# Batch 0's attention products as sixteen matmuls with tail rows copied, a filler behind the first, and batch 1's values loaded ahead of W2's last quarter

## The chip, the cores and the metric

The kernel runs on one core of a Trainium2 chip. The metric is device time in microseconds (us). Engines are written as the profile has them: PE is TensorE (PEld its weight loads), DVE is VectorE, ACT is ScalarE, POOL is GpSimd, SP is SyncE, whose queue issues transfers. Matmul results land in PSUM, in banks of 512 fp32 numbers per partition; everything else lies in SBUF, 128 partitions wide.

## What is computed

Sinkhorn attention over blocks, then a residual MLP with affine layers. Batch 4, 8 heads, sequence 768 in 8 blocks of 96, head size 64, so 512 channels.

```python
# sort_net P: five rounds of exp and of row and column normalization
k_sorted = np.einsum('bhij,bhjcd->bhicd', P, k_b)
v_sorted = np.einsum('bhij,bhjcd->bhicd', P, v_b)
scores = scale * np.matmul(q_b, k_sb.transpose(0, 1, 2, 4, 3))    # block by block, 96 x 96
attn = softmax(scores)
x = np.matmul(attn, v_sb)          # to (batch, 768, 512)
a1 = alpha1 * x + beta1
u = x + lam * np.einsum('ts,bsd->btd', w_tok, a1)
a2 = alpha2 * u + beta2
out = u + lam * (np.maximum(a2 @ w_ch1, 0.0) @ w_ch2)
```

## The kernel before

All four batches run through one program whose order is written out by hand: `Engine` (line 58) keeps the instructions of each engine in the order in which the Python code issues them (`tc.keep_in_program_order`, line 67), so nearly every instruction carries line 65. An engine that waits holds up everything behind it in its own queue. Waits come from data, and from buffers: a tile pool hands out a buffer again when its last reader is done. PSUM has two such pools: `psa`, two buffers of two banks each, and `psb`, four buffers of one bank each (lines 84 to 91). Which buffer a tile gets depends on how many were taken before it.

Batch 0 has a start of its own, written out in lines 900 to 985 and 1073 to 1082. In this order:

1. Values are mixed by the sort matrix (`v_mm`, `v_out`), and keys of head pairs 0 and 1 (`k_turn`, `k_copy`). The eight heads go in four pairs, g = 0 to 3.
2. `score(0, g, hf, ...)` multiplies queries with keys for four blocks, and ACT takes the exponentials into `et`. With a `psa` tile it is one activation of 768 elements, with `psb` tiles two of 384.
3. `pv_first(g)` (line 464) multiplies the exponentials of pair g with the values. Column 64 of the values is one, so each product carries its own row sum; DVE takes the reciprocal and multiplies, and the result is 128 channels of `x_of[0]`.
4. `wtok` turns the token weights (transposed on PE, copied by DVE or ACT into `w_tokT`); `first_mm(g)` multiplies them with x; `first_turn(g)` turns x itself; `first_finish` puts both together into `a2T`, the transposed input of the first channel product, on DVE (`SCALAR_TENSOR_TENSOR a2T`).
5. `h_part` and `h_unit` are the first channel product and its relu (`hTa`, `hTb` on ACT). `h_part(0, 0, m, [ci])` does one of the four chunks of 128 input channels, chunk ci being `a2T` of pair g = ci.

**How x lies.** A block has 96 rows, and later products want full tiles of 128 tokens. So tile kt (0 to 5) of `x` holds block kt in partitions 0 to 95, and 32 rows of block 6 or 7 in partitions 96 to 127. In `pv_first` a block of the first six is one matmul of 128 rows of weights (96 of them its own); blocks 6 and 7 are three matmuls of 32 columns each, which write straight to partitions 96 to 127 of the PSUM tile (lines 477 to 481). That makes 24 matmuls for a pair, one reciprocal over 12 numbers and one multiply of 128x768.

In batches 1 to 3 the same is done by `pv` (line 490): 16 matmuls in two halves, and `tails` (line 527) copies the rows of blocks 6 and 7 from `x[.., 6:8]` to partitions 96 to 127 by three DVE copies.

**Idle filling.** `slow(n)` (line 227) issues n matmuls of zeros in fp32, 128x512, which the hardware does in two passes each, into a `psa` tile that nobody reads. Before the change it is used ahead of the attention, never between attention products.

**Transfers.** The large loads are issued by POOL, in the order of the code: W1 in quarters, W2 in quarters (lines 956 and 957), then `load_kv(1)` (values, then keys of batch 1, each in two halves) and `load_q(1)` (lines 987 and 988). They share one DMA queue. `scale_weights(g)` (line 793) multiplies quarter g of W2 on DVE before the second channel product reads it; `put(b, hf, kind, n, ...)` names the step of the loop after which a function is run (line 1061: steps 10, 11, 12, 12). `mix_v(1, n, ...)` reads batch 1's values at steps 13 to 15.

Of the kernel before, what the change touches and what calls it, by code (L numbers as in the profile page):

```python
# [7 lines left out]
FT = mybir.dt.float32  # L8
# [3 lines left out]
ALU = mybir.AluOpType  # L12
# [4 lines left out]
def kernel(  # L17
# [22 lines left out]
    B, H, S, D = q.shape  # L40
    NB = sort_net.shape[-1]
    BLK = S // NB
# [44 lines left out]
    def psa(shape, dtype, name):  # L87
        return pools["psA"].tile(shape, dtype, name=name, tag="psA")

    def psb(shape, dtype, name):  # L90
        return pools["psB"].tile(shape, dtype, name=name, tag="psB")
# [100 lines left out]
                qn_of[b][:, kt, :, :], q[b, :, kt * 128:(kt + 1) * 128, :].rearrange("h p d -> p h d"),  # L192
            )

    def load_kv(b):
        for kv, src in ((1, v), (0, k)):
            raw = att.tile([128, HB, D], F16, name="raw", tag="raw", bufs=2)
            load_halves(raw, src[b])
            raw_of[(b, kv)] = raw
# [187 lines left out]
    def k_turn(b, g, ps):  # L387
        return turn_slab(k8, lambda r, g: bigK[b][r, g, :], g, "k_ps", ps)

    def k_copy(b, g, ps, half, eng):  # L390
        eng(
            KT0[:, g, :, :].rearrange("p i (th u) -> p (i th) u", th=2)[:, :, 0:HB].rearrange(
                "p x (c t) -> p x c t", t=12
            )[:, :, :, half * 6:half * 6 + 6],
            ps[half].rearrange("p (t x c) -> p x c t", t=6, c=4),
        )
# [17 lines left out]
    def score(b, g, hf, ps, fillers=0):  # L414
        if ps is psb:
            ps = [ps([128, 4 * BLK], FT, "sc_ps") for _ in range(2)]
            bank = [t_[:] for t_ in ps]
        else:
            ps = [ps([128, 2, 512], FT, "sc_ps")]
            bank = [ps[0][:, a, :] for a in range(2)]  # L420
        for _ in range(fillers):
            z = wz[:].bitcast(FT)[:, 0:192]
            pe.matmul(
                bank[0][:, 0:384], z[:, 0:128], z.unsqueeze(1).to_broadcast([128, 2, 192]), start=True, stop=True,
            )
        n = 128 if b == 0 else BLK
        keys = kT_of[b][:].rearrange("p g i t -> p (g i t)")
        for ii in range(4):
            i = 4 * hf + ii
            lo = (g * NB + i) * n  # L430
            w = min(128, H4 * NB * n - lo)
            for h2 in range(2):
                r = slice(h2 * 64, h2 * 64 + 64)
                pe.matmul(
                    bank[h2][0:w, ii * BLK:(ii + 1) * BLK], keys[r, lo:lo + w],
                    qT_of[b][r, g, i * BLK:(i + 1) * BLK], start=True, stop=True,
                )
        tag, bufs = ("ost", 4) if (b, g) == (0, 3) else ("et", 6)
        et = att.tile([128, 2, 4, BLK], F16, name="et", tag=tag, bufs=bufs)
        if len(ps) == 1:  # L440
            act.activation(
                et[0:n].rearrange("p a i t -> p a (i t)"), ps[0][0:n, :, 0:4 * BLK], AF.Exp, scale=scale
            )
        else:
            for a in range(2):
                act.activation(
                    et[0:n, a].rearrange("p i t -> p (i t)"), ps[a][0:n, :], AF.Exp, scale=scale
                )
        ets[(b, g, hf)] = et

    x_of = {}
# [12 lines left out]
    def pv_first(g):  # L464
        if g == 0:
            x_of[0] = moep.tile([128, 8, C], F16, name="x128", tag="x128", bufs=1)
        ps = psa([128, 2, 512], FT, "x_ps")[:, :, 0:480].rearrange("p a (k d) -> p a k d", d=80)
        for i in range(NB):
            for h2 in range(2):
                et = ets[(0, g, i // 4)][:].rearrange("p a i t -> p (a i t)")  # L470
                lo = (4 * h2 + i % 4) * BLK
                w = min(128, 8 * BLK - lo)
                val = Vs[:, (2 * g + h2) * NB + i, 0:D + 1]
                if i < 6:
                    pe.matmul(ps[0:w, h2, i, 0:D + 1], et[:, lo:lo + w], val, start=True, stop=True)
                else:
                    for a in range(3):
                        pe.matmul(
                            ps[96:128, h2, 3 * (i - 6) + a, 0:D + 1], et[:, lo + a * 32:lo + (a + 1) * 32], val,
                            start=True, stop=True,  # L480
                        )
        rc = att.tile([128, 2, 6], FT, name="rc", tag="rc", bufs=3)
        dve.reciprocal(rc[:], ps[:, :, :, D])
        dve.tensor_tensor(
            x_of[0][:, 0:NT, g * 128:(g + 1) * 128].rearrange("p k (a d) -> p k a d", a=2),
            ps[:, :, :, 0:D].rearrange("p a k d -> p k a d"),
            rc[:].rearrange("p a k -> p k a").unsqueeze(3).to_broadcast([128, NT, 2, D]), ALU.mult,
        )

    def pv(b, g, hf):  # L490
        if g == 0 and hf == 0:
# [35 lines left out]
    def tails(x, c):  # L527
        for a in range(3):
            dve.tensor_copy(x[96:128, a:a + 4:3, c], x[32 * a:32 * a + 32, 6:8, c])
# [88 lines left out]
    def row_sums(ps):  # L618
        ps = ps([128, 384], FT, "rr_ps")
        for ks in range(NT):  # L620
            j = ks % 4
            pe.matmul(
                ps[32 * j:32 * j + 32, :], ones[:], w_tokT[:, ks, 0:384], start=(ks < 4), stop=(ks > 1),
                skip_group_check=True,
            )
        act.copy(rrow[:], ps[:])
# [45 lines left out]
    def first_mm(g, ps):  # L672
        c = slice(g * 128, (g + 1) * 128)
        tps = tps_of[g] = ps([128, 384], FT, "tok_ps")[:]
        for ks in range(NT):
            pe.matmul(
                tps, x_of[0][:, ks, c], w_tokT[:, ks, 0:384], start=(ks == 0), stop=(ks == NT - 1),
            )
        if g == 3:
            first_finish(g)  # L680
        else:
            tok_copy(g)

    def first_turn(g, ps):
        c = slice(g * 128, (g + 1) * 128)
        ups = ps([128, 384], FT, "turn_ps")[:]
        for m in range(3):
            pe.matmul(
                ups[:, m * 128:(m + 1) * 128], x_of[0][:, m, c], ident16[:],
                start=(m == 0), stop=False, skip_group_check=True,  # L690
            )
        pe.matmul(ups, brow[:, c], rrow[:], start=False, stop=True, skip_group_check=True)
        if g == 0:
            z_of[0] = moep.tile([128, CT, 384], FT, name="z", tag="u32", bufs=3)
        act.activation(
            z_of[0][:, g, :], ups, AF.Identity, bias=ab2col[:, CT + g:CT + g + 1], scale=ab2col[:, g:g + 1],
        )
        if g < 3:
            first_finish(g)
# [51 lines left out]
    def h_part(b, hf, m, cis):  # L751
        if b not in hAB_of:
            hAB_of[b] = tuple(
                moep.tile([128, HK, 512], F16, name=n, tag=n, bufs=1) for n in ("hTa", "hTb")
            )
        if (b, hf) not in hT_of:
            hT_of[(b, hf)] = [
                hAB_of[b][m // HK][:, m % HK, hf * 128:hf * 128 + 384] for m in range(HT)
            ]
        if cis[0] == 0:  # L760
            h_of[m] = psb([128, 384], FT, "h_ps")
        for ci in cis:
            pe.matmul(
                h_of[m][:], W1p[:, ci, m * 128:(m + 1) * 128], a2T_of[b][hf][:, ci, :],
                start=(ci == 0), stop=(ci == CT - 1),
            )
        if cis[-1] == CT - 1:
            act.activation(hT_of[(b, hf)][m], h_of[m][:], AF.Relu)
# [128 lines left out]
    def wtok(ks, eng):  # L897
        prep_wtok(ks, 0, psb, eng)
# [55 lines left out]
        pool.dma_start(W1p[:, :, g * 512:(g + 1) * 512], w1v[:, :, g * 512:(g + 1) * 512])  # L954
    permute(1, pool.tensor_copy, 0, 6)
    for g in range(4):
        pool.dma_start(W2p[:, g * 4:(g + 1) * 4, :], w2v[:, g * 4:(g + 1) * 4, :])
    moe_start(0)
    a1_of[0] = moep.tile([128, 8, C], F16, name="a1", tag="a1", bufs=1)
    pv_first(0)  # L960
    kp2 = k_turn(0, 2, psb)
    kp3 = k_turn(0, 3, psb)
    for g, kp in ((2, kp2), (3, kp3)):
        k_copy(0, g, kp, 0, copy)
        k_copy(0, g, kp, 1, act.copy)
    score(0, 2, 0, psa)
    score(0, 2, 1, psb)
    pv_first(1)
# [3 lines left out]
        wtok(ks, copy)  # L972
    wtok(4, act.copy)
    wtok(5, copy)
    first_mm(0, psb)
    pv_first(2)
    row_sums(psb)
    first_mm(1, psb)
    first_turn(0, psb)
# [4 lines left out]
    first_turn(2, psa)  # L984
    scale_affine(betaB)

    load_kv(1)
    load_q(1)
    pool.memset(Vs[0:BLK, :, D:GRP], 1.0)

# [67 lines left out]
        put(b, 0, "h", 4, lambda b=b: moe_cross(b, 1))  # L1058
        put(b, 0, "c", 2, lambda b=b: moe_affine(b, 1))

    for g, m in enumerate((10, 11, 12, 12)):
        put(0, 0, "h", m, lambda g=g: scale_weights(g))
    for n, at_ in enumerate(((0, 1, "c", 4),) * 3 + ((0, 1, "c", 5),) * 3 + ((0, 1, "c", 6),) * 2):
        put(*at_, lambda n=n: block_weights(n))
# [7 lines left out]

    for m in range(3):
        h_part(0, 0, m, [0])
    first_turn(3, psa)
    first_mm(3, psa)
    for ci in (1, 2):
# [55 lines left out]
```

## Time and profile before

| | |
|---|---|
| time, median of 3 runs | 256.55 us (255.8 to 257.79) |
| the profiled execution's own time | 256.33 us |
| its span, first to last instruction | 254.6 us |
| busy: PE, DVE, ACT, POOL | 96%, 68%, 61%, 18% of the span |
| mean granted clock of PE | 0.993 |
| the stage that the change touches | some 18.5 to 37 us |

Columns of a timeline: start, length, engine, line, operation, tile written <- tile read, shape, count. This is PE's part of the stage, where pairs 0 and 1 are done:

```profile
18.58 1.02 PE L65 MATMUL x_ps<-Vs,et 128*128 128x65 f16 x24
19.53 0.21 PE L65 MATMUL k_ps<-bigK,k 64*64 64x64 f16 x1
21.22 0.94 PE L65 MATMUL k_ps<-bigK,k 64*64 64x64 f16 x47 [1.48 <-ACT et L65]
22.54 0.63 PE L65 MATMUL sc_ps<-qT,kT 64*128 64x96 f16 x16 [0.37 <-DVE kT L65]
23.09 1.64 PE L65 MATMUL x_ps<-Vs,et 128*128 128x65 f16 x24
```

The times of an execution are those of one run; PE's matmuls are pipelined, so a group's length is a little more than what it takes of PE. In brackets stands the idle time before a group and what ended it. A granted clock of 0.50 in a stretch means that the matmuls in it take twice as long.

### The profile page before, as it was taken

To read this page: it belongs to the slowest core of one execution; us is meant where nothing else is said; L and a number is where in the kernel's file an instruction comes from. 1 tells how busy PE (TensorE), PEld (TensorE's weight loads), DVE (VectorE), ACT (ScalarE), POOL (GpSimd) and SP (SyncE) were. 2 spreads that over 40 slices of the span, in tenths; PEclk is the share of its full clock that TensorE was granted. 3 is DMA by queue.
4 is the path that set the end of the run, shared out by engine and by line. 5 is a ranking of instruction groups with operands and counts; after the bars stand their busy time and mean duration, and the time that the engine had idled before them with its cause. 6 is when DMAs were issued, how large, how long until landed. Compare 5 with 4: busy or idle time off the path is not lost.

```text
span 254.6 us, 6059 instructions
## 1 busy us (share of the span) xinstructions
PE 244.0 (96%) x2416; PEld 159.7 (63%) x2416; DVE 174.1 (68%) x461; ACT 155.7 (61%) x285; POOL 46.1 (18%) x70
## 2 busy tenths in 40 slices
PE   7897999999999999999999999999999999999994
PEld 2475765555465545556765797558756875686783
DVE  5884588667379868279896685398978862462773
ACT  4796675567788679786564696878364005837400
POOL 8699604000082010191000010000000000000000
PEclk9997999999999999999999999999999999999999
DMA  5999999998999997999961179710203132111023
GB/s 98 202 210 192 207 205 210 216 179 197 165 179 180 131 209 124 178 159 164 136 161 39 31 189 127 141 23 0 85 0 66 50 115 45 21 41 44 0 85 82
DMA packets 61936, 31.09 MB, mean 122 GB/s; under 512 B 50562, under 2 KB 57618, under 8 KB 61908
## 3 DMA queue, kind: packets, MB, share of 16 engines
q0 software_dynamic: 20976, 16.91, 45.7%
q1 hardware_dynamic: 40836, 13.76, 32.0%
q8 instruction: 19, 0.31, 0.5%
q14 instruction: 9, 0.07, 0.1%
q10 hardware_dynamic: 96, 0.03, 0.1%
HBM read 32.79 MB, written 8.65 MB: 163 GB/s over the span
## 4 chain that ended last, share of the span: by engine, by line
PE 77%; DVE 9%; ACT 6%; DMA 3%; issue 2%; POOL 1%; DVEq 0%; ACTq 0%; POOLq 0%
PE h_ps L65 28%; PE tok_ps L65 12%; PE px L65 8%; PE ch_ps L65 8%; PE pz L65 6%; PE py L65 5%; DMA v<-in_v_dram 3%; PE x_ps L65 3%; DVE x L65 3%; PE sc_ps L65 2%; DVE sums L65 2%; PE kmix_ps L65 2%; PE mix_ps L65 2%; ACT kT L65 1%; ACT vd L65 1%
## 5 line engine op out<-in xcount | busy, mean ns | idle before, releaser
L65 PE MATMUL h_ps<-a2T,W1p 128*128 128x384 bf16 x512 | 93.4, 326 | 0.3 <-DVE a2T L65 0.3
L65 PEld LDWEIGHTS <-W1p 128*128 128x128 bf16 x512 | 47.8, 98 | 30.7
L65 ACT ACTIVATE hTa<-h_ps 128x384 f16<-128x384 f32 x64 | 31.2, 490 | 30.6 <-PE h_ps L65 29.5
L65 ACT ACTIVATE hTb<-h_ps 128x384 f16<-128x384 f32 x64 | 31.3, 489 | 8.7 <-PE h_ps L65 8.7
L65 DVE SCALAR_TENSOR_TENSOR u<-tok_ps,x 128x512 f32<-128x512 f32 x21 | 14.5, 692 | 27.0 <-PE tok_ps L65 27.0
L65 PE MATMUL tok_ps<-a,w_tokT 128*128 128x512 f16 x126 | 30.3, 379 | 0.0
L65 ACT CAST kT<-kmix_ps 64x512 f16<-64x512 f32 x36 | 25.7, 713 | 7.0 <-PE kmix_ps L65 6.5
L65 ACT ACTIVATE et<-sc_ps 96x768 f16<-96x768 f32 (+2 forms) x36 | 24.6, 736 | 2.4 <-PE sc_ps L65 2.4
L65 ACT CAST u<-u 128x512 f16<-128x512 f32 x21 | 13.0, 618 | 20.4 <-DVE u L65 20.4
L65 PEld LDWEIGHTS <-sums 128*128 128x128 f16 x216 | 21.1, 98 | 3.8 <-issue 0.7
L65 PEld LDWEIGHTS <-hTa 128*128 128x128 f16 x192 | 18.2, 98 | 6.6
L65 PEld LDWEIGHTS <-hTb 128*128 128x128 f16 x200 | 18.5, 98 | 6.1
L65 PEld LDWEIGHTS <-w_tokT 128*128 128x128 f16 x126 | 12.3, 98 | 13.1 <-DVE a L65 0.3
L65 DVE TENSOR_TENSOR x<-x_ps,rcb 96x512 f16<-96x512 f32 x24 | 16.5, 687 | 0.8
L65 DVE TENSOR_TENSOR sums<-hTa,hTb 128x512 f16<-128x512 f16 (+2 forms) x27 | 8.9, 330 | 10.3 <-ACT hTb L65 10.0
L65 PEld LDWEIGHTS <-et 96*128 96x128 f16 (+4 forms) x288 | 12.6, 103 | 2.7
L65 DVE SCALAR_TENSOR_TENSOR ost<-px,u 128x256 f32<-128x256 f32 x27 | 11.3, 419 | 3.4 <-PE px L65 3.4
L65 PE MATMUL x_ps<-Vs,et 96*128 96x65 f16 (+4 forms) x288 | 13.5, 199 | 0.0
L65 PE MATMUL ch_ps<-W2p,hTa 128*128 128x512 f16 x48 | 11.9, 380 | 0.0
L65 PE MATMUL ch_ps<-W2p,hTb 128*128 128x512 f16 x48 | 11.7, 379 | 0.0
L65 POOL DMA_DIRECT2D qn<-in_q_dram x12 | 10.7, 915 | 5.2 <-DMA raw<-in_v_dram 4.8
L65 PE MATMUL sc_ps<-qT,kT 64*128 64x96 f16 (+1 forms) x256 | 10.0, 210 | 1.5 <-DVE x L65 0.7
(140 smaller groups left out, 351.2 us busy)
## 6 DMA issues: line engine op xcount, KB each, us to landing
out_dram<-ost SPq DMA_DIRECT2D x23, 192.0 KB, 2.4
raw<-in_v_dram POOLq DMA_DIRECT2D x6, 384.0 KB, 8.4
raw<-in_k_dram POOLq DMA_DIRECT2D x6, 384.0 KB, 10.8
Vs<-vscr SPq DMA_DIRECT2D x3, 768.0 KB, 7.9
W1p<-in_moe_w_ch_dram POOLq DMA_DIRECT2D x4, 512.0 KB, 11.6
W2p<-in_moe_w_ch_dram POOLq DMA_DIRECT2D x4, 512.0 KB, 15.6
qn<-in_q_dram POOLq DMA_DIRECT2D x12, 128.0 KB, 11.1
vscr<-mixed POOLq DMA_DIRECT2D x4, 384.0 KB, 5.0
```

Source lines behind the costliest of these rows:

```text
L65: ins = getattr(self.eng, name)(*args, **kwargs)
```

## The change

- `load_kv` takes the kinds to load; values of batch 1 are issued ahead of W2's last quarter, keys where both were.
- `pv_first` does blocks 6 and 7 like the others, into a second PSUM tile `xt_ps` out of `psb`. That makes 16 matmuls. DVE takes two reciprocals and two multiplies, on 96 partitions, and writes `x_of[0][0:96, 0:8]`.
- `first_tails(g)` calls `tails` (unchanged) for pair g: three DVE copies of 32x256. Its place in the order is written out: for pair 0 behind the key copies of pairs 2 and 3, for pair 1 behind the copies of the token weights, for pair 2 right behind `pv_first(2)`, for pair 3 behind `scale_affine(betaB)` and the first three `h_part`, ahead of `first_turn(3)`.
- One `slow(1)` follows `pv_first(0)`.
- The scaling of W2's last quarter goes from step 12 to step 15. No other DVE instruction lies between the two places, so DVE's order stays as it is.

```diff
-    def load_kv(b):
-        for kv, src in ((1, v), (0, k)):
+    def load_kv(b, *kvs):
+        for kv in kvs or (1, 0):
+            src = (k, v)[kv]
...
         ps = psa([128, 2, 512], FT, "x_ps")[:, :, 0:480].rearrange("p a (k d) -> p a k d", d=80)
+        tl = psb([128, 320], FT, "xt_ps")[:].rearrange("p (a k d) -> p a k d", a=2, d=80)
         for i in range(NB):
             for h2 in range(2):
...
-                if i < 6:
-                    pe.matmul(ps[0:w, h2, i, 0:D + 1], et[:, lo:lo + w], val, start=True, stop=True)
-                else:
-                    for a in range(3):
-                        pe.matmul(
-                            ps[96:128, h2, 3 * (i - 6) + a, 0:D + 1], et[:, lo + a * 32:lo + (a + 1) * 32], val,
-                            start=True, stop=True,
-                        )
-        rc = att.tile([128, 2, 6], FT, name="rc", tag="rc", bufs=3)
-        dve.reciprocal(rc[:], ps[:, :, :, D])
-        dve.tensor_tensor(
-            x_of[0][:, 0:NT, g * 128:(g + 1) * 128].rearrange("p k (a d) -> p k a d", a=2),
...
-        )
+                dst = ps[0:w, h2, i, 0:D + 1] if i < 6 else tl[0:w, h2, i - 6, 0:D + 1]
+                pe.matmul(dst, et[:, lo:lo + w], val, start=True, stop=True)
+        rc = att.tile([128, 2, NB], FT, name="rc", tag="rc", bufs=3)
+        dve.reciprocal(rc[0:BLK, :, 0:6], ps[0:BLK, :, :, D])
+        dve.reciprocal(rc[0:BLK, :, 6:8], tl[0:BLK, :, :, D])
+        for lo, src in ((0, ps), (6, tl)):
+            n = 6 - 2 * lo // 3
+            dve.tensor_tensor(
+                x_of[0][0:BLK, lo:lo + n, g * 128:(g + 1) * 128].rearrange("p k (a d) -> p k a d", a=2),
+                src[0:BLK, :, :, 0:D].rearrange("p a k d -> p k a d"),
+                rc[0:BLK, :, lo:lo + n].rearrange("p a k -> p k a").unsqueeze(3).to_broadcast([BLK, n, 2, D]), ALU.mult,
+            )
+
+    def first_tails(g):
+        tails(x_of[0], slice(g * 128, (g + 1) * 128))
...
     for g in range(4):
+        if g == 3:
+            load_kv(1, 1)
         pool.dma_start(W2p[:, g * 4:(g + 1) * 4, :], w2v[:, g * 4:(g + 1) * 4, :])
...
     pv_first(0)
+    slow(1)
     kp2 = k_turn(0, 2, psb)
     kp3 = k_turn(0, 3, psb)
     for g, kp in ((2, kp2), (3, kp3)):
         k_copy(0, g, kp, 0, copy)
         k_copy(0, g, kp, 1, act.copy)
+    first_tails(0)
     score(0, 2, 0, psa)
...
     wtok(5, copy)
+    first_tails(1)
     first_mm(0, psb)
     pv_first(2)
+    first_tails(2)
     row_sums(psb)
...
-    load_kv(1)
+    load_kv(1, 0)
     load_q(1)
...
-    for g, m in enumerate((10, 11, 12, 12)):
+    for g, m in enumerate((10, 11, 12, 15)):
         put(0, 0, "h", m, lambda g=g: scale_weights(g))
...
     for m in range(3):
         h_part(0, 0, m, [0])
+    first_tails(3)
     first_turn(3, psa)
     first_mm(3, psa)
```

More of the change, by code (lines that the diff above doesn't have):

```diff
@@ L473, in pv_first @@
                 val = Vs[:, (2 * g + h2) * NB + i, 0:D + 1]
-                if i < 6:
-                    pe.matmul(ps[0:w, h2, i, 0:D + 1], et[:, lo:lo + w], val, start=True, stop=True)
-                else:
-                    for a in range(3):
-                        pe.matmul(
-                            ps[96:128, h2, 3 * (i - 6) + a, 0:D + 1], et[:, lo + a * 32:lo + (a + 1) * 32], val,
-                            start=True, stop=True,
-                        )
-        rc = att.tile([128, 2, 6], FT, name="rc", tag="rc", bufs=3)
-        dve.reciprocal(rc[:], ps[:, :, :, D])
-        dve.tensor_tensor(
-            x_of[0][:, 0:NT, g * 128:(g + 1) * 128].rearrange("p k (a d) -> p k a d", a=2),
-            ps[:, :, :, 0:D].rearrange("p a k d -> p k a d"),
-            rc[:].rearrange("p a k -> p k a").unsqueeze(3).to_broadcast([128, NT, 2, D]), ALU.mult,
-        )
+                dst = ps[0:w, h2, i, 0:D + 1] if i < 6 else tl[0:w, h2, i - 6, 0:D + 1]
[12 more added lines that the diff above has]
+        tails(x_of[0], slice(g * 128, (g + 1) * 128))
     def pv(b, g, hf):
```

## The prediction

> **What bounds the kernel now.** The page's chain says PE 77%, and from 41 us on it is matmuls almost throughout, with short waits for ScalarE and VectorE and none for a transfer; so whatever the change gains or loses before 41 us reaches the end whole, unless a transfer comes to have the last word. The change lies between 18.5 and 37 us, so I took the chain again for 16 to 45 us (start, length, what):
>
> ```profile
> 20.31 0.91 issue
> 21.22 0.59 PE k_ps L65 x23
> ...
> 28.09 0.76 PE x_ps L65 x21
> ...
> 30.86 0.57 ACT z L65
> 31.43 0.02 issue
> 31.45 0.62 DVE a2T L65
> ...
> 33.12 0.61 DVE a2T L65
> 33.73 0.60 DVE alphaB L65
> 34.33 0.53 DVE a2T L65
> 34.85 0.60 DVE betaB L65
> ```
>
> Two things are to be seen. At 19.6 to 21.2 TensorE stands still. From 31.45 to 36.1 the chain runs on VectorE, which goes from one operation straight to the next; matmuls wait for it. Then the busy time of each engine in stretches of 3.41 us, cut where the granted clock changes (columns: stretch and length, busy us of PE, PEld, DVE, ACT, POOL with instruction counts, granted clock, DMA share, GB/s):
>
> ```profile
> 12.56:15.97 3.41, 2.83 (x152) 2.71 (x153) 3.27 (x7) 3.41 (x7) 3.41 (x4) 1.00 1.15 207
> ...
> 19.39:22.80 3.41, 1.56 (x68) 1.31 (x66) 2.16 (x4) 1.77 (x5) 3.41 (x4) 1.00 1.20 165
> 22.80:26.21 3.41, 3.41 (x60) 2.94 (x54) 1.46 (x4) 2.59 (x6) 3.41 (x5) 0.50 1.16 220
> 26.21:29.62 3.41, 3.41 (x53) 2.45 (x51) 1.83 (x7) 2.05 (x4) 3.02 (x5) 1.00 1.24 205
> ...
> 33.04:36.45 3.41, 3.11 (x23) 1.85 (x22) 3.03 (x6) 1.92 (x4) 0.00 (x0) 1.00 1.24 206
> ```
>
> A stretch with PE busy 1.56 of 3.41 us (46%) is followed by a whole one at half clock; one with 2.83 (83%) is not. VectorE has 1.9 us free at 22.8 to 26.2, and 0.4 at 33.0 to 36.5. Last, three tail copies in batch 1, with POOL quiet and with POOL issuing DMAs:
>
> ```profile
> 80.28 0.69 DVE L65 COPY x<-x 32x256 f16<-32x256 f16 x3
> ...
> 111.63 1.28 DVE L65 COPY x<-x 32x256 f16<-32x256 f16 x3
> ```
>
> **Matmuls.** Each pv_first drops from 24 to 16 matmuls. At full clock the first one's 24 took 1.02 us with starts 0.03 apart, so 8 fewer save 0.25; the last of the first group still ends near 19.5, because its new tail bank waits for the exponential that ends at 19.16. The second group now costs 1.57, at half clock; 16 at full clock take 0.51 (the row of batch 1).
>
> **VectorE.** Per group, now: reciprocal 0.26 from start to start and a 128x768 multiply 0.88, together 1.14. After: two reciprocals 0.45, a 96x768 multiply 0.88, a 96x256 one (0.35: from 0.61 for 96x512 and 0.88 for 768 elements, 0.27 per 256), and three copies 0.70: 2.4. That is 1.25 more, four times.
>
> **The filler.** Two passes of 0.43 plus its start, some 1.05 us (the earlier ones end 0.95 after they begin). It covers 19.3 to 20.35 of the stall. What ends the stall? The waits table blames ScalarE's exponentials (1.5 us), but the half that the waiting matmul needs ended at 19.54. The DMA view of 18.5 to 21.5 has one instruction packet of 16 KB, and the weight load's own idle time there, 1.59 us, is put down to issue, not to an engine. I read it as a late instruction fetch, which a filler doesn't hasten: TensorE resumes at 21.22 again, only with 6 more key matmuls done (0.1 us). Bounds: 0 gained, or 0.87 if the stall goes with the filler. I take 0.1, because the packet is what the trace shows. The Trainium skill (Runtime: NRT & Kernel Launch, Instruction fetch mechanics) says that blocks of 256 instructions are fetched ahead and that the cost is mostly hidden; by that the stall is something else, and the rival in which it goes with the filler is the likelier one.
>
> The filler lifts the 46% stretch to about 2.5 us (72%). That lies between 46 and 83; I take it that the clock holds.
>
> **Schedule to 27 us.** Keys copied at 22.3 (22.4 now), scores 22.43 to 22.88, second group 22.9 to 23.4 (24.7 now). But bank order shifts by one with the tail tiles, and the scores of head pair 3 now take a PSUM bank that an exponential of pair 2 has to read first: ScalarE starts with pair 2 at 22.87, 0.70 for the whole one and 0.52 for the half in that bank, to 24.1. So they start at 24.15 (24.66 now): of 1.3 us gained only 0.5 is left. Tail copies of group 0 fit before 23.45, beside POOL's weight issues (22.1 to 23.55): 0.70, or 1.28 by the row above, of which all but 0.1 is slack later. VectorE finishes group 1 at 25.2, the w_tok copies at 26.8; the first token product runs 26.33 to 27.30, against 26.95 to 27.92: 0.65 earlier.
>
> **Schedule to 37 us.** Group 2 is read by VectorE from 27.88 to 29.63, its tails to 30.36. z(0) ends at 30.50 (31.41 now), a2T(0) at 31.15. Here the third token product waits for a2T(0), whose bank it takes: 31.2 (31.68 now). Group 3: VectorE 31.06 to 32.80, then a2T(1) at 32.73 (33.12 now), alphaB 33.26, a2T(2) 33.86, betaB 34.39 (34.77 now): 0.4 ahead. Then group 3's tails, 34.99 to 35.68. They stand behind betaB in VectorE's queue, and first_turn(3) waits for each of them; TensorE idles from 33.55 to 35.28. Queued behind it are first_mm(3) and every h matmul of the other three input chunks. first_turn(3) and first_mm(3) take 1.30 now (33.94 to 35.24) and end at 36.93, so a2T(3) starts at 37.2 instead of 35.51: 1.7 us late. Now these 1.30 us of matmuls lie beside a2T(2) and betaB; after, they come behind both and behind 0.70 of copies. Everything of h, and VectorE's a1 products behind a2T(3), moves with it.
>
> **The clock again.** On the same grid, 33.04 to 36.45 would hold 0.16 of h, 0.68 of first_turn(3) and 0.49 of first_mm(3): 1.3 of 3.41 us, 39%, below the 46% that was followed by half clock. Then 36.45 to 39.87 runs at half: up to 1.7 us lost, some 0.2 hidden by the 0.43 of PE idle of 33.0 to 39.9: 1.5.
>
> **Loads.** Values of batch 1 ahead of W2's last quarter on POOL: both are issued by 31.8 instead of 31.7, on a queue that stays full. A value half takes 1.85 us of it, a quarter 2.5. The quarter lands at 49.9 instead of 46.1; its scaling runs at 53.8 now, in the same place of VectorE's queue (its slot moves, but nothing lies between). The values land at 47.4 instead of 49.9, and the first mix reads them at 50.8. Cost nothing; if the quarter came 4 us later still, it would begin to cost.
>
> **Sum.** Against the profiled run's 256.33 (span 254.6, 1.7 around it; 0.2 under the median 256.55): +1.7 for the late a2T(3), with the gains before it already inside, +0.1 for copies beside POOL, +1.5 for the clock: 259.6.
>
> **Rivals.** *The clock holds after 36 us*: +1.8, 258.1. For it: the grid may lie otherwise in other runs; with a stretch starting before 31.6 or after 33.8, none falls under 46%. Against: the 2.2 us of starts between them are most of the 3.4, and the limit may be higher than 46%. The Trainium skill (TensorE: Matmul & The Clock Gate, Why this matters for your kernels) has a rule that gives this result: the clock drops after idle gaps of over about 3 us, and here the longest is 1.7. The trace disagrees: it dropped behind 46% busy with no gap over 1.5.
>
> *The stall at 21.2 goes with the filler*: all moves 0.85 forward, TensorE idles less, 257.2 with the clock held. Against: the packet.
>
> *TensorE is the bound, and VectorE's extra 5 us hide*: VectorE sits idle 1.46, 0.97, 1.92, 1.54 and 1.26 us before its pieces from 19.6 to 31.5. Then the half clock (1.7), the stall (0.87) and 0.25 of matmuls come off: 253.5, faster. It decides at a2T(3): it would have to start before 35.5, and the tails of group 3 have no idle time ahead of them.
>
> *The filler fails to hold the clock at 22.8*: the 0.65 gained by 27.3 becomes 0.25, 260.0, and with copies at 1.28 some 260.6.
>
> **Chances.** Forecast 0.53, a tenth of it under 259.1; clock holds 0.20; stall goes 0.12; TensorE bound 0.08; filler fails 0.07. A measurement here tells about 1%, 2.6 us. Slower by more (over 259.1): 0.48 + 0.07 = 0.55. Within: 0.05 + 0.20 + 0.12 + 0.01 = 0.38. Faster: 0.07. Range 256.9 to 260.9: it takes in the forecast (its own range 258.9 to 260.4), the clock rival and the stall rival, and leaves out 0.08 for TensorE bound and some 0.08 at the edges.
>
> **What would show it.** Right: first_turn(3) waits for VectorE's copies of x for 1.5 us or more near 34 us, a2T(3) starts near 37.2, a row of clock 0.50 behind it and none at 22.8 to 26.2; TensorE still stalls up to 21.2. Wrong: a2T(3) at 35.5 or earlier, scores of pair 3 before 24 us, or PE waiting for W2 or the values near 50 us.

## The result, and the profile after

The changed kernel is slower: 264.40 us (median of 262.36, 264.04, 264.77 and 265.31) against 257.12, ratio 1.0279 (95% interval 1.0202 to 1.0356). The forecast was 259.6, at most 260.9: the direction was right, the size less than half of what came. The profiled execution is the fastest of the four, 262.36 us with a span of 260.6, 6.03 more than the 256.33 us that the kernel before took in its profile. The medians in this document are of all executions, the ratios leave out those over 1.5% above the fastest of the same kernel, so a ratio can differ a little from the quotient of two medians.

This is the chain of waits of the changed kernel for 16 to 45 us (start, length, what; "issue" is idle time for which the profile shows no cause):

```profile
19.86 2.29 DVE ab2col L65
...
25.05 0.22 DVE x L65
25.27 0.01 issue
25.28 0.59 DVE x L65
...
35.53 0.60 DVE alphaB L65
36.13 0.53 DVE a2T L65
36.66 0.61 DVE betaB L65
37.27 0.02 issue
37.29 0.23 DVE x L65
37.52 0.05 issue
37.57 0.23 PE turn_ps L65
...
38.46 0.99 PE tok_ps L65 x6
...
39.55 0.63 DVE a2T L65
```

The same stage in the timelines, VectorE's `a2T` of pairs 1 and 3 of the kernel before:

```profile
33.12 0.61 DVE L65 SCALAR_TENSOR_TENSOR a2T<-tok_ps,ab2col,z 128x384 bf16<-128x384 f32 x1
...
35.51 0.62 DVE L65 SCALAR_TENSOR_TENSOR a2T<-tok_ps,ab2col,z 128x384 bf16<-128x384 f32 x1
```

and those of the changed kernel, with TensorE's first_turn(3) between them:

```profile
34.93 0.60 DVE L65 SCALAR_TENSOR_TENSOR a2T<-tok_ps,ab2col,z 128x384 bf16<-128x384 f32 x1
...
37.57 0.73 PE L65 MATMUL turn_ps<-ident,x 128*128 128x128 f16 x3 [1.66 <-DVE x L65]
...
39.55 0.62 DVE L65 SCALAR_TENSOR_TENSOR a2T<-tok_ps,ab2col,z 128x384 bf16<-128x384 f32 x1 [1.53 <-PE tok_ps L65]
```

The lower part of the chain is the forecast's: pair 3's copies behind betaB, then first_turn(3) and first_mm(3), then a2T(3), which starts at 39.55 instead of 35.51. The upper part was not forecast: a multiply of 128x4 numbers (ab2col) holds the chain for 2.29 us, where a pair of them took 0.35 before, and pair 0's tail copies, foreseen before 23.45, run at 25.0 to 26.1. The delay against the kernel before is 1.81 us at a2T(1) and a2T(2), 4.03 at a2T(3), still 4.03 at 94 us, 5.69 at 128 and 6.04 at 213.

The busy time of each engine in stretches of 3.41 us of the changed kernel (columns as before: PE, PEld, DVE, ACT, POOL with counts, granted clock, DMA share, GB/s):

```profile
20.14:23.55 3.41, 2.68 (x59) 1.64 (x55) 3.38 (x6) 2.59 (x6) 3.41 (x5) 1.00 1.19 161
...
33.79:37.20 3.41, 1.93 (x13) 0.93 (x11) 3.41 (x6) 1.51 (x3) 0.00 (x0) 1.00 1.25 206
37.20:40.62 3.42, 3.01 (x21) 1.84 (x22) 1.34 (x5) 1.09 (x2) 0.00 (x0) 1.00 1.24 206
```

VectorE is full in the first two of these. Behind the emptier one of TensorE, 1.93 of 3.41 us, the clock held here, against the forecast. The other three executions had mean clocks of 0.977, 0.985 and 0.987 (0.997 in this one) and spans of 263.5, 262.3 and 263.0.

### The profile page after: what moved, and what is told of

Its sections match the earlier page's. It is cut to its first block, busy times and chain, and to the rows that moved or that the text cites. A ratio compares the mean times of both kernels' runs of the same rounds, so it can differ in the third digit from the quotient of the medians.

```text
span 260.6 us, 6018 instructions
## 1 busy us (share of the span) xinstructions
PE 246.1 (94%) x2386; PEld 158.8 (61%) x2386; DVE 182.0 (70%) x481; ACT 155.8 (60%) x285; POOL 46.1 (18%) x70
## 4 chain that ended last, share of the span: by engine, by line
PE 75%; DVE 15%; ACT 3%; DMA 3%; issue 2%; SPq 1%; DVEq 0%; POOLq 0%
PE h_ps L65 28%; PE tok_ps L65 12%; PE px L65 8%; PE pz L65 5%; PE py L65 5%; PE ch_ps L65 5%; DVE x L65 4%; PE x_ps L65 2%; DMA q<-in_q_dram 2%; PE sc_ps L65 2%; PE q_ps L65 2%; PE mix_ps L65 1%; SPq L65 1%; DVE sums L65 1%; PE kmix_ps L65 1%
## 5 line engine op out<-in xcount | busy, mean ns | idle before, releaser
L65 DVE COPY x<-x 32x256 f16<-32x256 f16 x48 | 12.2, 254 | 1.0
L65 PEld LDWEIGHTS <-et 96*128 96x128 f16 (+3 forms) x256 | 11.1, 101 | 2.6 <-issue 0.2
L65 ACT CAST mixed<-mix_ps 128x1024 f16<-128x1024 f32 x9 | 9.2, 1017 | 3.6 <-PE mix_ps L65 3.6
```

The lines of the kernel that those rows point to most:

```text
L65: ins = getattr(self.eng, name)(*args, **kwargs)
```

## The experiments

Each ratio is to runs of the kernel before on the same chip, with its 95% interval.

| kernel | median, us | ratio |
|---|---|---|
| attention_alone | 262.97 | 1.0178 (1.0121 to 1.0235) |
| filler_alone | 257.45 | 0.9987 (0.9949 to 1.0026) |
| loads_alone | 257.64 | 1.0000 (0.9967 to 1.0034) |
| after_again | 263.42 | 1.0236 (1.0183 to 1.0288) |
| tails0_later | 261.57 | 1.0142 (1.0095 to 1.0189) |
| tails3_early | 261.73 | 1.0173 (1.0130 to 1.0217) |
| both_moved | 258.84 | 1.0080 (1.0049 to 1.0112) |
| no_tails | 256.86 | 0.9997 (0.9969 to 1.0025) |
| wp_later | 261.56 | 1.0167 (1.0128 to 1.0206) |
| idle_filled | 263.41 | 1.0259 (1.0217 to 1.0301) |
| wp_later_tails3_early | 258.76 | 1.0079 (1.0055 to 1.0104) |
| wp_later_filled | 259.98 | 1.0100 (1.0068 to 1.0131) |

### One part of the change at a time

*attention_alone*: the changed kernel without `slow(1)` behind `pv_first(0)` and with the loads and the scaling as before.

> The attention part of the change on the kernel before: sixteen matmuls, tail tile and tail copies as in the changed kernel, without the filler and without the moved loads. Theory A (the loss is VectorE's: four groups of extra operations, and above all the tail copies of pair 3 behind betaB, so that first_turn(3), first_mm(3) and a2T(3) come late): a2T(3) starts at 37.5 to 39.6 us as in the changed kernel, and the time is 260 to 264 us. Rival B (the loads: values of batch 1 ahead of W2's last quarter move the transfers of later batches, which cost 1.7 us at 82 to 105 us in the changed kernel's profile): 258.5 to 261, and a2T for batch 1's first half behind the uT transposes waits no longer than in the kernel before (0.66 us). Rival C (the filler, with the shifted first 10 us): within 1% of the kernel before.

Ratio 1.0178, most of the loss. Its profiled execution, one of the two longest of six (265.92 us), had three stretches at half clock, so a2T(3) came only at 42.79, later than expected; with the shorter ones it can't be compared row by row. The delay behind 94 us, which rival B gives to the loads, is there without them: 1.5 us more by 128 us.

*filler_alone*: the kernel before with one line more.

```diff
     pv_first(0)
+    slow(1)
```

> One slow(1) behind pv_first(0) in the kernel before, nothing else. Theory A: the stretch that is 46% busy fills to some 70%, no half clock at 22.8 to 26.2 us, and 0 to 1.5 us are gained: 255 to 256.6 us; as in the changed kernel's profile, no stall up to 21.2 us is put down to issue. Rival C (the filler takes a PSUM buffer and time of PE that the attention needs, and brings the slow start, TensorE at half speed up to 9.9 us instead of 5.7): 258 to 260 us.

Ratio 0.9987, no change. The half clock at 22.8 us is gone as expected and the first product with the token weights starts 0.7 earlier, at 26.23. But TensorE still stops for issue ahead of 21.2, which was not expected (0.36 us, up to 20.69, inside the filler), and again for 0.48 us, up to 27.52, and a2T(0) is only 0.07 earlier. The gain that was expected did not come.

*loads_alone*: `load_kv(1, 1)` ahead of W2's last quarter, the scaling at step 15; nothing else of the change.

> Only the values of batch 1 ahead of W2's last quarter, and its scaling three steps later. Theory A: no change, 255.5 to 257.5 us; a2T behind the uT transposes at 100 us waits 0.7 us as before. Rival B: the later transfers shift, that a2T waits 1.5 to 2.5 us, and the time is 258 to 259 us.

Ratio 1.0000. The moved loads cost nothing.

*after_again*: the changed kernel, unedited.

> The changed kernel as it is, for a second profile. If TensorE's cold start up to 9.9 us (5.7 in the kernel before) belongs to the run and not to the change, it may be back at 5.7 here, and then VectorE's ab2col takes some 0.35 us instead of 2.56. If the half clock that I forecast behind 36 us comes in the runs of lower mean clock, and this profile is of one of them (clock under 0.99), a row of 0.50 stands between 33 and 43 us. Time 262 to 265.5 us.

Full clock again came late, from 9.64 us on (5.73 in the kernel before), and no stretch after that was at half clock. The pair of ab2col took 0.35 this time, but its place was taken. The timeline of this second profile (start, length, engine, operation, tile written <- read, shape, count; in brackets the idle time before):

```profile
23.52 2.62 DVE L65 COPY x<-x 32x256 f16<-32x256 f16 x3
26.18 0.23 DVE L65 RECIPROCAL rc<-x_ps 96x12 f32<-96x12 f32 x1
...
27.81 0.86 PE L65 MATMUL wtok_ps<-ident,wp 128*128 128x128 f16 x9 [1.42 <-DVE x L65]
...
23.57 2.26 POOL L65 COPY wp<-wt 128x1728 f16<-128x1728 f16 x2
```

Three copies that take 0.70 alone take 2.62 here, next to POOL's copy of wp. In single rows: POOL's copy is two, of 1.64 us (to 25.21) and 0.69 (to 25.83); VectorE's first copy takes 1.79 and ends at 25.31, its second 0.59 and ends at 25.91, its third, with POOL done, takes 0.22. So each of the two ends some 0.09 us after one of POOL's. What is queued behind them, the reciprocals of pair 1, starts at 26.18, though TensorE had delivered at 24.3; TensorE then waits 1.42 us for VectorE. In the first profile the same thing struck ab2col, 2.36 us for 128x4 numbers beside POOL's first copy of wp (19.87 to 22.11).

### The tail copies: moved, or left out

*tails0_later*:

```diff
-    first_tails(0)
     score(0, 2, 0, psa)
...
     score(0, 3, 1, psa)
+    first_tails(0)
     for ks in range(4):
```

> The changed kernel with pair 0's tail copies two places later in VectorE's order: behind pv_first(1), ahead of the copies of the token weights. Theory A (VectorE's three copies of 32x256 are held up while POOL copies wp, 23.5 to 25.8 us: 2.62 us in the second profile of the changed kernel, 3.15 us with the attention part alone, 0.70 when POOL is quiet, and pv_first(1)'s reads wait behind them): here they fall behind 25.8 us and take 0.70 to 0.9 us, the first product of token weights starts 0.8 to 1.2 us earlier (27.5 to 27.9 with a start like that of the second profile, 28.6 there), and the median falls by 1 to 2.5 us, to 261 to 262.5. Rival D (the copies cost what they cost; it is the extra VectorE work of 2.1 us per pair that delays, wherever it stands): no change, 263 to 264.5 us.

The median came as expected, with a ratio of 1.0142; its interval lies below that of the changed kernel in its first set and overlaps that of after_again by a hair. The copies took 1.31 from 25.84 on, beside POOL's DMA issues, more than expected, and the first token product starts at 28.11, 0.5 earlier instead of 0.8 to 1.2.

*tails3_early*:

```diff
     pv_first(3)
+    first_tails(3)
     first_turn(1, psb)
...
-    first_tails(3)
     first_turn(3, psa)
```

> The changed kernel with pair 3's tail copies right behind pv_first(3), ahead of alphaB, betaB and two a2T, instead of behind them. Theory A (their place behind betaB puts 0.70 of copies and then 1.30 to 1.98 of matmuls of first_turn(3) and first_mm(3) one after the other, ahead of a2T(3)): a2T(3) follows betaB with an idle time under 0.3 us (1.53 in the changed kernel), 1.5 us earlier, the stretch of TensorE idle time at 36 to 37.6 us goes, and with it the half clock behind it in some runs: median 260 to 262.3 us. Rival E (the copies only push the other a2T and the h products behind them, the same 1.5 us later): 263 to 264.5 us.

VectorE's part of its timeline, where the last line had an idle time of 1.53 us ahead of it in the changed kernel (shown above) and has none now:

```profile
35.09 0.69 DVE L65 COPY x<-x 32x256 f16<-32x256 f16 x3
35.81 0.62 DVE L65 SCALAR_TENSOR_TENSOR a2T<-tok_ps,ab2col,z 128x384 bf16<-128x384 f32 x1
...
37.47 0.68 DVE L65 SCALAR_TENSOR_TENSOR betaB<-lamB,betaB 128x512 f16<-128x512 f32 x1
38.22 0.62 DVE L65 SCALAR_TENSOR_TENSOR a2T<-tok_ps,ab2col,z 128x384 bf16<-128x384 f32 x1
```

a2T(3) starts 1.3 us earlier than in the changed kernel; the median is again as expected; the ratio, 1.0173, has an interval that overlaps the changed kernel's, so this move alone isn't settled by its times.

*both_moved*: both edits.

> Both moves in one. Theory A: they add up, 258.5 to 261 us, 0.5 to 1.5% above the kernel before, which is what is left of the extra VectorE work. Rival D and E: over 262 us.

1.0080, well clear of the changed kernel: the two places together are worth about 1.5%, 4 us. a2T(3) starts at 37.19, 1.68 later than in the kernel before.

*no_tails*: without the four calls of `first_tails`; rows 96 to 127 of batch 0's x are set to zero once instead.

> The changed kernel without any tail copies: rows 96 to 127 of batch 0's x stay zero, set once by POOL at some 10 us, where it waits for a transfer. It leaves out the copies and nothing else. Theory A (the copies, above all those of pairs 0 and 3, are the loss; the smaller matmul count and the filler make up for the 0.55 us that the split reciprocal and multiply add per pair): 255.5 to 258.5 us, within 1% of the kernel before. Rival D (the loss is all of the added VectorE work, or the transfers): 260 us or more.

0.9997, with a2T(3) at 35.54, 0.03 later than before. So the copies are the whole loss, and the sixteen matmuls with all their extra reciprocals and multiplies, the filler and the loads come out even. Of the 4.03 us at a2T(3), by these profiles some 2.35 hang on the two places, and the 1.68 that both_moved keeps are what the copies cost in better ones. Why no gain, when 32 matmuls and the half clock are gone? TensorE's timeline of this kernel:

```profile
20.43 0.31 PE L65 MATMUL k_ps<-bigK,k 64*64 64x64 f16 x7
21.16 0.85 PE L65 MATMUL k_ps<-bigK,k 64*64 64x64 f16 x41 [0.42 <-issue]
...
27.40 0.22 PE L65 MATMUL xt_ps<-Vs,et 128*128 128x65 f16 x2
28.20 0.23 PE L65 MATMUL xt_ps<-Vs,et 128*128 128x65 f16 x2 [0.58 <-issue]
```

Both stops end 1.3 to 1.5 us after a 16 KB packet of instructions has landed (19.81 and 26.69); so do those of the kernel before (19.70, to 21.22) and of filler_alone (19.28, to 20.69; 25.98, to 27.52). That fits a wait for instructions; no run varies the packets, so it isn't shown. The 0.9 us that this kernel is ahead at the first token product melts to 0.29 at a2T(0), and VectorE's second reciprocal and multiply for pair 3 (0.33 us more than before) take the rest: a2T(1) is 0.03 late.

### POOL's copy moved instead

*wp_later*: VectorE's order is the changed kernel's.

```diff
-    permute(1, pool.tensor_copy, 0, 6)
     for g in range(4):
         if g == 3:
+            permute(1, pool.tensor_copy, 0, 6)
             load_kv(1, 1)
```

> The changed kernel with POOL's second copy of wp behind the issue of three quarters of W2 instead of ahead: it moves from 23.5 to some 25.8 us, the loads 2.2 us forward; VectorE's order is the changed kernel's. Theory A (the copies of pair 0 wait for POOL's copy of wp): the three take 0.7 to 1.1 us in their old place, the second reciprocal pair starts near 24.8 instead of 26.2 us, and the median falls by 1 to 2 us, to 261 to 262.7, as when the copies themselves were moved. VectorE's reads of PSUM beside the moved copy keep their length (0.95 for 96x768). Rival D (position in VectorE's order, or the copies themselves): no change, 263 to 264.5.

Ratio 1.0167 and a median within what was expected; the interval overlaps that of after_again a little. The timeline, VectorE's and POOL's rows:

```profile
22.78 1.04 DVE L65 COPY x<-x 32x256 f16<-32x256 f16 x3
23.85 0.23 DVE L65 RECIPROCAL rc<-x_ps 96x12 f32<-96x12 f32 x1
...
26.79 1.97 DVE L65 COPY x<-x 32x256 f16<-32x256 f16 x3
...
35.50 0.72 DVE L65 COPY x<-x 32x256 f16<-32x256 f16 x3
38.91 0.62 DVE L65 SCALAR_TENSOR_TENSOR a2T<-tok_ps,ab2col,z 128x384 bf16<-128x384 f32 x1 [2.69 <-PE tok_ps L65]
...
26.18 2.25 POOL L65 COPY wp<-wt 128x1728 f16<-128x1728 f16 x2
```

With POOL's copy gone from 23.6, pair 0's copies take 1.04 and the reciprocals follow at 23.85, sooner than expected; in idle_filled, whose first exponentials come as early (17.4 against 17.6), they follow at 26.19. With POOL's copy now at 26.18, pair 1's take 1.97 instead of 0.72, so the move only shifts the collision to a place where it costs less. VectorE's multiply of 96x768 out of PSUM takes 0.92 beside POOL's first copy (at 19.98) and 0.95 with POOL not copying, so it is not touched. This shows the cause from the other side: where POOL copies, VectorE's copies stretch.

It shows the end of the forecast too. a2T(1) and a2T(2) start 0.02 later than in the kernel before, and a2T(3) 3.40. The busy time of the two stretches there:

```profile
32.87:36.28 3.41, 1.52 (x11) 0.58 (x9) 3.26 (x9) 1.14 (x2) 0.00 (x0) 1.00 1.24 207
36.28:39.69 3.41, 3.41 (x12) 1.72 (x13) 0.62 (x1) 0.79 (x2) 0.00 (x0) 0.50 1.24 206
```

TensorE is busy for 1.52 us (45%) in the stretch in which it waits for pair 3's copies, and the next stretch, with first_mm(3), runs at half clock.

*idle_filled*: the changed kernel, with that wait filled.

```diff
     first_tails(3)
+    slow(1)
     first_turn(3, psa)
```

> The changed kernel with one slow(1) more, ahead of first_turn(3), in the 1.66 us in which TensorE waits for pair 3's tail copies. Theory F (that idle time and the earlier one at 25 to 27.8 us let the clock fall to half in some runs, which is what separates the runs of 264 to 265 us from those of 261 to 262): a stretch there is filled to over 60%, no run's mean clock is under 0.985 for its sake, and the median falls by 0.5 to 2 us. Rival (the spread comes from elsewhere, from the first 10 us or from the transfers of 82 to 105 us): clocks from 0.977 to 0.999 as before, median 263 to 265.

A miss: 1.0259, not under the changed kernel. Its stretches behind pair 0's copies, which took 3.22 us here:

```profile
22.95:26.36 3.41, 2.35 (x49) 1.66 (x43) 3.35 (x5) 3.15 (x6) 3.41 (x4) 1.00 1.16 214
26.36:29.77 3.41, 1.95 (x13) 1.43 (x13) 3.17 (x11) 0.48 (x1) 2.30 (x5) 0.50 1.25 205
```

The half clock lasts from 26.4 to 33.2, ahead of the filler's place, where the code is still the changed kernel's: TensorE waits 2.02 us for VectorE up to 27.82, and a2T(3) starts at 41.78, 2.2 later than in the changed kernel's two profiles. No mean clock was under 0.985, but that gained nothing that shows.

*wp_later_filled*: the same line in wp_later, where TensorE has no other wait over 0.4 us between 21.3 and 40 us.

> POOL's second copy of wp later, and one slow(1) ahead of first_turn(3). In the profile without this slow(1), TensorE was 1.52 of 3.41 us busy (45%) from 32.87 to 36.28 us, the next stretch ran at half clock, a2T(3) started at 38.91 and the tenth h matmul at 40.12. Theory F (that idle stretch is what costs the half clock, worth 1.3 us at a2T(3) and 1.8 at the h matmuls): the stretch holds 2.3 to 2.6 us of PE, no 0.50 behind it, a2T(3) starts at 37.2 to 37.8, and the median falls by 1 to 2 us from 261.56, to 259.5 to 260.6. Rival (the clock falls here for another reason, or the filler only takes its place): 261 to 262.5.

Its stretches:

```profile
31.86:35.27 3.41, 2.77 (x16) 1.39 (x14) 3.41 (x8) 1.81 (x3) 0.75 (x1) 1.00 1.23 203
35.27:38.68 3.41, 2.57 (x15) 1.31 (x15) 1.78 (x6) 0.67 (x1) 0.00 (x0) 1.00 1.24 207
```

No half clock, mean clocks of 0.998 to 1.000 in all twelve runs (0.990 to 0.993 in five of wp_later's six), and 259.98 us, 1.0100: 1.6 less than wp_later, by ratios whose intervals just touch. a2T(3) came at 38.40, later than expected, since pair 1's copies took 2.58 us this time.

*wp_later_tails3_early*: wp_later with tails3_early's edit and `scale_affine(betaB)` behind `first_mm(3, psa)`.

> POOL's second copy of wp later, pair 3's tail copies right behind pv_first(3), and betaB behind first_mm(3). Theory A: tail copies then neither wait for POOL nor stand between TensorE and a2T(3); a2T(3) starts 0 to 0.8 us later than in the kernel before (36 to 37.2 us with a start like that of the changed kernel's second profile), and the time is 256.5 to 258.5, no better than the kernel before, since without any copies it was 0.9997 of it. Rival: 259 or more.

1.0079, just above what was expected, no better than both_moved. a2T(3) starts at 37.20, 1.69 later than in the kernel before where 0 to 0.8 were expected: pair 1's copies, now beside POOL's, take 2.96 us. No version here beats the kernel before, and without any copies there was nothing to gain.

## Why the prediction was wrong in its size

**The step that failed** is "Tail copies of group 0 fit before 23.45, beside POOL's weight issues: 0.70, or 1.28 by the row above, of which all but 0.1 is slack later". With POOL's copy of wp where the changed kernel has it, from 23.5 to 25.8 us, they start between 22.9 and 25.1 in four profiles (after, after_again, tails3_early, idle_filled) and end at 26.1 or 26.2 in all of them. Even where they start at 22.94, ahead of POOL's copy (idle_filled), they end no sooner. VectorE's work for pair 1 follows 1.4 us later than before instead of ahead of it, and a2T(1) is 1.81 late instead of 0.4 early: 2.2 us. The trace of before showed POOL's two copies at these times; I read POOL's row for its DMA issues alone, and the 1.9 us that VectorE had free at 22.8 to 26.2 as time that a copy can use:

```profile
19.91 2.24 POOL L65 COPY wp<-wt 128x1728 f16<-128x1728 f16 x2
...
23.55 2.24 POOL L65 COPY wp<-wt 128x1728 f16<-128x1728 f16 x2
```

The Trainium skill (SBUF — State Buffer, Who interferes with whom) has the rule: VectorE's copies can run in a mode that uses a pair of SBUF ports which is GpSimd's too, and then one engine blocks the other for the whole instruction; an operation with two inputs in SBUF contends with a GpSimd operation that reads there. The trace agrees (1.79 for a copy of 0.22, 2.36 for a multiply of 0.16); by that rule and POOL's row of before, an estimate of the term is up to 2.2 us, the length of POOL's two pieces.

**Pair 3's copies: right.** first_turn(3) waits 1.66 us for them, and from a2T(2) to a2T(3) the delay grows by 2.2, where the forecast had 2.1 (from 0.4 ahead to 1.7 behind).

**The clock behind 36 us: shown in wp_later, not in the changed kernel.** The changed kernel's two profiles do not have it, wp_later's does, where the delay is 3.90 at the tenth h matmul, 1.7 more than the serial 2.2. Filling the gap takes it away there. In the changed kernel the runs of lower clock are the longer ones, but filling the same gap gained nothing (idle_filled), whose half clock stands behind pair 0's copies instead. One stretch of half clock lowers the mean to 0.993 (the profile of before), so by an estimate the runs at 0.977 to 0.987 have two or more of them, where the forecast had one; which gaps bring them in the changed kernel stays open. The rule of the Trainium skill (TensorE: Matmul & The Clock Gate, Why this matters for your kernels) that gave the rival, a drop behind gaps of over some 3 us, does not hold here either: the longest gap in wp_later's stretch is 1.66.

**The filler, the stall and TensorE as the bound.** In no_tails and wp_later, where TensorE is early enough, the stall stayed as forecast: seven key matmuls get ahead of it, the rest go at 21.2. In the changed kernel's own profiles, whose first exponentials come 0.9 to 1.9 us later, there is none to see. The filler holds the clock at 22.8. But most of the 0.65 us that this was to bring by 27.3 is taken back by a second stop for issue at 27.0 to 28.2, in filler_alone and no_tails, so it is worth nothing. That also disposes of the rival in which TensorE is the bound: with all copies gone the time is 0.9997.

**The loads: right**, 1.0000 alone.

**What the sum lacked.** In the profile 1.66 us more come in between 94 and 128 us. SyncE's queue, of the kernel before and then of the changed one:

```profile
82.97 8.30 SPq L65 DMA_TRANSPOSE qT<-qn  x6
...
94.46 4.26 SPq L65 DMA_TRANSPOSE uT<-u  x3
```

```profile
87.55 10.94 SPq L65 DMA_TRANSPOSE qT<-qn  x6
...
99.69 4.77 SPq L65 DMA_TRANSPOSE uT<-u  x3
```

The transposes of batch 2's queries take 2.6 us longer, those of u start late, and TensorE waits for the a2T behind them (1.16 us). In after_again this term is 0.4, in filler_alone, with nothing shifted before it, 1.2, in loads_alone and no_tails none; filler_alone's twelve runs show no loss on the mean. It varies with how transfers meet; what decides it stays open.

Worked against the profile's 262.36: 2.2 for pair 0's copies, less 1.5 for the clock, plus 2.0 behind 94 us, 0.3 of it still later, makes 2.7 of the 2.76 that the forecast was short. That it was short by no more is in part luck: the 1.5 for a half clock that did not come hide as much of what was missing. Against the median, 2.0 us more, the profile lacks the runs at lower clock.

## What to carry to other kernels

Before an SBUF-to-SBUF copy or a two-input operation goes to VectorE, look at what POOL *computes* in that stretch, not at how busy VectorE is: here three copies of 0.70 us took up to 3.2. Moving POOL's copy instead helps only if its new place is free of such operations too: in wp_later it met pair 1's copies. Do not put work between an operation that must wait for the matrix engine and the matmuls that it waits for; and count the busy share of TensorE in 3.41 us stretches around each new wait, since a short wait can cost half the clock of the stretch behind it. Where instruction supply or another engine sets the pace next, saved matmuls and a saved clock bring nothing.

## What was not expected of the hardware

- A VectorE copy that starts first can still lose: in after_again it starts at 23.52, POOL's at 23.57, and it ended at 25.31, behind POOL's first copy. POOL had been issuing a DMA until then. In the first profile one that starts at 25.05, 0.03 ahead of POOL's second piece, took its usual 0.22. Beside a DMA issue of POOL's such a copy takes up to 0.57 instead of 0.22 (tails0_later, wp_later).
- When the clock first goes up differs between executions whose first instructions are almost the same. In five profiles the stretch before it began at 2.82 to 3.07 us and held 2.58 to 2.72 us of TensorE, and the full clock came one stretch later, at 9.6 to 9.9; in six it began at 2.15 to 2.70, held 2.70 to 3.25, and the full clock came at 5.6 to 6.1; the other three had it at 4.5, 4.6 and 6.7. This delayed the first exponentials by up to 2.0 us, yet a2T(3) by nothing (39.55 and 39.59 in the two profiles of the changed kernel, with exponentials 0.8 apart), since pair 0's copies end with POOL's. All five are of kernels with the tail copies and the filler, which lie far behind, but others of these kernels are among the nine; what decides it stays open.
- The busy time of a stretch does not give the limit for the drop exactly: 1.66 of 3.41 us held the clock in tails0_later, 1.52 in wp_later and 1.65 in attention_alone did not, and 2.35 in idle_filled did not either.
